# Five weight buffers, a later half of the first weights, and two pairs of heads in rounded parts

## The chip, the cores and the metric

The kernel runs on one core of a Trainium2 chip. The metric is the time of one launch in microseconds (us) as the device measures it; several runs are taken and their median is given. A profiled execution is a run of its own, and its time and its span (from the first to the last instruction) stand beside the median.

## The reference

Causal attention with a decay, for 4 batches, 8 heads, 576 rows and a head size of 64, and behind it two dense layers over all 2304 tokens (model width 512, hidden width 2048):

```python
scores = scale * np.matmul(q, k.transpose(0, 1, 3, 2))
cum = np.cumsum(np.log(np.clip(f, 0.0001, 1.0)), axis=-1)
decay = cum[:, :, :, None] - cum[:, :, None, :]
scores = np.where(causal, -1000000000.0, scores + decay)
attn = softmax(scores)
x = np.matmul(attn, v)            # then (tokens, 512)
x = np.maximum(x @ w_in, 0.0) ** 2 @ w_out
x = elu(x @ w_in2) @ w_out2
```

All of it is in float32.

## The kernel before, in words

**Two ways to multiply.** TensorE multiplies float32 as it is ("plain"), or two rounded parts of each operand: a high part in the rounded type F32R and the rest. With parts, a product is two or three matmuls over the parts. Making the parts costs copies and subtractions on the other engines.

**Attention.** The rows of a batch are cut at row 256. Kind "A" of a pair of heads is rows 0 to 255, kind "4" the last 64 rows of both heads together, and kind "B" rows 256 to 511 (with the last 64 rows joined in at the product with v). `todo` (lines 632 to 639) is the list of these items. For batch 0 (`SPLIT`) all eight A items come first, then for each of the four pairs the items 4, B, B; for the other batches each pair is A, A, 4, B, B. For an item `soft` makes the scores on TensorE, the row minimum of the negated scores on VectorE (line 315) and the exponential on ScalarE (line 318); one item later `outs` transposes (line 379) and multiplies with v (lines 383 and 386). The decay comes in as up to four more rows of q and k, taken from the tile `ca` for the first 256 rows and from `aug`, a table in DRAM, for the others (`aug_rows`, line 259).

**Batch 0 is plain** (`PLAIN`, lines 44 and 225). `fetch_plain` (line 232) brings the operands straight to where TensorE reads them: for A one `rawA` tile per pair (lines 237 to 242, three buffers of tag `raw`, so the fourth pair waits for the first), with two small transfers of decay rows from `ca` (line 240); for B a `rawB` and a `rawC` tile. `load_head` (line 266) has nothing to do for batch 0. For other batches `fetch_head` brings `raw` (800 KB, line 230), and `load_head` makes the parts `qk1` and `qk2` and `vv`: copies on ScalarE, VectorE and GpSimd, subtractions on GpSimd (`ENG`, line 46).

**The first dense layer** is done in two halves of the hidden width. During attention, `unit(u)` (line 572) computes the first half for 256 tokens; unit 0 can start when the A items of batch 0 are stored, and `moe_step` lets out one piece at a time by a credit per item (`PACE`, `COST`). Its weights, 8 slices of `w_in` and then 8 of `w_out`, are loaded by `load_w` (line 128): a transfer of 512 KB into one of two buffers `raws_w` (line 135), an Abs on ScalarE (line 141), four steps on VectorE that round a 64-bit number to float32 (lines 142 to 145; the tile is `wt`), then the high part on ScalarE (line 146) and the low part on GpSimd (line 147, `WL`). `W_AT` (line 36) says how many of these 16 weights are let out at each item.

**The order.** The kernel is written as a loop over the items (line 688). At item i it fetches for items up to i + 4 (`FETCH`), loads up to i + 2 (`AHEAD`), then weights, then scores, then the product with v of the item before, with pieces of the dense layer between. A planner orders the instructions of each engine by this order and by its own estimate of when operands are there, so an instruction whose operands are ready can be placed ahead of an earlier one that waits; a buffer is given out when its last reader is done. All transfers go out from SyncE's queue (SP), in one order. From the end of attention (`at.close()`, line 732) the rest of the first layer and the second layer follow.

Of the kernel before, what the change touches and what calls it, by code (L numbers as in the profile page):

```python
# [10 lines left out]
F32 = mybir.dt.float32  # L11
F32R = mybir.dt.float32r
I32 = mybir.dt.int32
# [3 lines left out]
B, H, S, D = 4, 8, 576, 64  # L17
# [7 lines left out]
RAW = QW + S  # L25
ALL = RAW + 5 * D
# [6 lines left out]
W_MAX = float(np.uint32(0x47EFFE00).view(np.float32))  # L33
PACE = (1.4, 0.9, 1.85, 1.75)
COST = {'A': 0.7, '4': 1.1, 'B': 1.7}
W_AT = (1, 1, 1, 1, 1, 1, 1, 1, 2, 2, 2, 2)
W_FIRST = 0
AHEAD = 2
FETCH = 4
LAG = 1  # L40
# [1 line left out]
SPLIT = (0,)  # L42

PLAIN = (0,)
CP = {'pA': 'a', 'pB': 'av', 'xA': 'a', 'xB': 'a'}
ENG = {'qk': 'aaa', 'ql': 'ppp', 'kh': 'pvv', 'kl': 'ppp', 'vh': 'ppp', 'vl': 'ppp', 'xl': 'pv'}
NORM = 'ap'
# [4 lines left out]
DEPTH1 = 2  # L52
ORD2 = (3, 0, 1, 2, 4)
AUG0 = 2
AUG_AT = 3
DELAY = 0
MEM = "gpsimd"
# [7 lines left out]
def f32(ap):  # L65
    return ap.bitcast(F32)
# [10 lines left out]
def attention_then_moe_kernel(ctx, tc, first, firstv, plain, qkv, aug0, f, w1, w2, out):  # L77
    nc = tc.nc
# [46 lines left out]
    def less(dst, x, hi):  # L125
        nc.gpsimd.tensor_tensor(out=dst, in0=x, in1=f32(hi), op=ALU.subtract)  # L126

    def load_w(src, m, fc, wp, i, late):
        if i == 0:
            wslot[m, fc] = wp.tile([128, 2, 1024], F32R, tag=f"w{fc}", name=f"w{m}_{fc}")  # L130
        w = wslot[m, fc]
        if late:
            raw = xb.tile([128, 512, 2], I32, tag="wraw", name="wraw")
        else:
            raw = raws_w[:, n_raw[0] % 2]
            n_raw[0] += 1
        nc.sync.dma_start(out=raw, in_=src[fc, i].bitcast(I32).rearrange("p (n t) -> p n t", t=2))
        lo, hi = raw[:, :, 0], raw[:, :, 1]
        t = xa.tile([128, 512], I32, tag="o", name="wt")
        wh, wl = (w[:, r, i * 512:(i + 1) * 512] for r in range(2))  # L140
        nc.scalar.activation(out=f32(t), in_=f32(hi), func=AF.Abs)  # L141
        nc.vector.tensor_scalar(f32(t), f32(t), W_MIN, W_MAX, op0=ALU.max, op1=ALU.min)  # L142
        nc.vector.tensor_scalar(t, t, 3, 0x3FFFFFFF, op0=ALU.logical_shift_left, op1=ALU.bitwise_and)
        nc.vector.scalar_tensor_tensor(t, hi, -0x40000000, t, op0=ALU.bitwise_and, op1=ALU.bitwise_or)
        nc.vector.scalar_tensor_tensor(t, lo, 29, t, op0=ALU.logical_shift_right, op1=ALU.bitwise_or)  # L145
        nc.scalar.activation(out=wh, in_=f32(t), func=AF.Copy)
        minus(WL[late][i], wl, f32(t), wh)

# [30 lines left out]
    nc.sync.dma_start(out=fr, in_=f)  # L179
    x0 = xa.tile([128, 2 * NC, CH], F32R, tag="xu", name="x0")  # L180
    raws_w = xa.tile([128, 2, 512, 2], I32, tag="xu", name="raws_w")
    qk2s = [a1.tile([128, RAW], F32R, name=f"qk2_{i}") for i in range(BUFS["qs"])]
    mz = a1.tile([128, 512], F32, name="mz")
    m4 = a1.tile([128, 288], F32, name="m4")
    ptA = [[a1.tile([128, 512], F32R, name=f"ptA{s}{t}") for t in range(2)] for s in range(2)]
# [29 lines left out]
    for k in range(2):  # L215
        mask(m4[64 * k:64 * k + 64, 224:288], [[-1, 64]])

    n_load = [0]

    raws = {}  # L220

    pairs = {}

    def fetch_head(b, h, part):
        if b in PLAIN:
            fetch_plain(b, h, part)
            return
        raw = ab.tile([128, ALL], F32, tag="raw", name="raw", bufs=BUFS["raw"])
        raws[b, h, part] = raw
        nc.sync.dma_start(out=raw, in_=qkv[b, h])  # L230

    def fetch_plain(b, h, part):
        g = b * H + h
        k = h % 2
        if part == "A":
            if k == 0:
                t = ab.tile([128, ALL], F32, tag="raw", name="rawA", bufs=BUFS["raw"])
                nc.sync.dma_start(out=t[0:64, 0:1024], in_=first[h // 2])
                for i in range(2):
                    nc.sync.dma_start(out=t[64:68, 512 * i:512 * i + 512], in_=f32(ca[g + i:g + i + 1]))  # L240
                nc.sync.dma_start(out=t[:, 1024:1280], in_=firstv[h // 2])
                pairs[b, h // 2] = t
            t = pairs[b, h // 2]
            raws[b, h, part] = Plain(t, 512 * k - Q0, 512 * k + 256, t[:, 1024 + 128 * k:1152 + 128 * k].rearrange("p (j d) -> p j d", d=D))
            return
        if k == 0:
            t = ab.tile([128, ALL], F32, tag="raw", name="rawB", bufs=BUFS["raw"])
        else:
            t = hd.tile([128, RAW], F32, tag="qk1", name="rawC", bufs=BUFS["qs"])
        nc.sync.dma_start(out=t[0:64, 0:RAW], in_=plain[h])  # L250
        nc.sync.dma_start(out=t[64:68, 0:RAW], in_=aug[g])
        if k == 0:
            v = t[:, RAW:ALL]
        else:
            v = hd.tile([128, 5 * D], F32, tag="vv", name="vp", bufs=BUFS["vv"])
        nc.sync.dma_start(out=v, in_=qkv[b, h, :, RAW:ALL])
        raws[b, h, part] = Plain(t, 0, QW, v.rearrange("p (j d) -> p j d", d=D))

    def aug_rows():
        cp, cn = (ab.tile([32, 2, S - 256], F32R, tag="eb", name=t, bufs=BUFS["eb"]) for t in ("cp", "cn"))  # L260
        split_c(cp, cn, slice(256, S))
        for rows, c0, src in ((slice(0, 2), Q0, ca[:, 0:2, 0:256]), (slice(2, 4), QW, ca[:, 2:4, 256:512]),
                              (slice(0, 2), 0, cp[:, :, 0:256]), (slice(0, 2), Q4, cp[:, :, 256:]), (slice(2, 4), QW + 256, cn)):
            nc.sync.dma_start(out=aug[:, rows, c0:c0 + src.shape[2]], in_=f32(src))

    def load_head(b, h, part):
        q0, q1, k1, js = {"F": (0, QW, S, 5), "A": (Q0, QW, 256, 2), "B": (0, Q0, S, 5)}[part]
        w = "ABF".index(part)
        raw = raws.pop((b, h, part))
        if b in PLAIN:  # L270
            return raw
        v0 = QW + 256 if part == "A" else RAW
        vr = raw[:, v0:v0 + js * D].rearrange("p (j d) -> p j d", d=D)
        qk1 = hd.tile([128, RAW], F32R, tag="qk1", name="qk1", bufs=BUFS["qs"])
        qk2 = qk2s[n_load[0] % len(qk2s)]
        n_load[0] += 1
        kc = slice(QW, QW + k1)
        qc = slice(q0, q1)
        g = b * H + h
        if part == "A":  # L280
            ac = slice(Q0, QW + 256)
            copy(ENG["qk"][w], qk1[:, ac], raw[:, ac])
        else:
            ac = slice(0, RAW)
            if part == "F":
                copy(ENG["qk"][w], qk1, raw[:, ac])
            else:
                copy(ENG["qk"][w], qk1[:, qc], raw[:, qc])
                copy(ENG["qk"][w], qk1[:, kc], raw[:, kc])
        if part == "A":  # L290
            nc.sync.dma_start(out=f32(qk2[64:68, ac]), in_=f32(ca[g:g + 1]))
        else:
            nc.sync.dma_start(out=f32(qk2[64:68, ac]), in_=aug[g, :, ac])
        minus(ENG["ql"][w], qk2[0:64, qc], raw[0:64, qc], qk1[0:64, qc])
        if ENG["kh"][w] == "d":
            nc.sync.dma_start(out=f32(qk2[0:64, kc]), in_=f32(qk1[0:64, kc]))
        else:
            copy(ENG["kh"][w], qk2[0:64, kc], f32(qk1[0:64, kc]))
        minus(ENG["kl"][w], qk1[64:128, kc], raw[64:128, kc], qk1[64:128, kc])
        vv = hd.tile([128, 5, 2 * D], F32R, tag="vv", name="vv", bufs=BUFS["vv"])  # L300
        copy(ENG["vh"][w], vv[:, 0:js, 0:D], vr)
        minus(ENG["vl"][w], vv[:, 0:js, D:2 * D], vr, vv[:, 0:js, 0:D])
        return qk1, qk2, vv
# [306 lines left out]
    def drain(gen):  # L610
        for _ in gen:
            pass
# [46 lines left out]
    wl = weights(1, w1, wa, range(8), False, True)  # L659

    wait = [0]

    def moe_step():
        for u in range(NU):
            if units[u] is None:
                continue
            if not started[u] and not ready(u):
                return False
            if not started[u] and u:
                if wait[0] < DELAY:  # L670
                    wait[0] += 1
                    return False
            started[u] = True
            wait[0] = 0
            if HOLD is not None and len(trail) > HOLD:
                with tc.issue_after(trail[-1 - HOLD].ins):
                    left = next(units[u], "end") != "end"
            else:
                left = next(units[u], "end") != "end"
            if left:  # L680
                return True
            units[u] = None
        return False

    credit = 0.0
    for _ in range(W_FIRST):
        next(wl)
    for i in range(len(todo) + LAG):
        if i == AUG0:
            nc.sync.dma_start(out=aug, in_=aug0)  # L690
        if i == AUG_AT:
            aug_rows()
        while fetches and fetches[0][0] <= i + FETCH:
            fetch_head(*fetches.pop(0)[1:])
        while loads and loads[0][0] <= i + AHEAD:
            load(*loads.pop(0)[1:])
        if i < len(todo):
# [217 lines left out]
```

## Time and profile before

| what | value |
|---|---|
| median of 3 runs (lowest to highest) | 1060.36 us (1059.25 to 1060.42) |
| profiled execution: its time, its span | 1061.57 us, 1059.8 us |
| mean granted TensorE clock | 0.998 |
| busy in the span: TensorE, its weight loads | 1027.7 us (97%), 873.6 us (82%) |
| busy in the span: VectorE, ScalarE, GpSimd | 621.3, 491.8, 228.2 us |
| moved by DMA | 115.48 MB, 109 GB/s over the span |

The profiled execution lies 1.2 us above the median of the runs. PE is TensorE's matmuls, PEld its weight loads, DVE VectorE, ACT ScalarE, POOL GpSimd, SP SyncE; SPq is an issue on SyncE's queue. A plain float32 matmul stands as two records in the trace. The end of a matmul is modelled, so in a run of matmuls the distance from one group's start to the next group's start tells more than the duration of one.

### The profile page before, as it was taken

Reading aid. Unit: us, or ns where it says so; the run is one execution under the profiler, and the core shown is the slowest. Engines: PE = TensorE matmul, PEld = TensorE weight load, DVE = VectorE, ACT = ScalarE, POOL = GpSimd, SP = SyncE. Lnnn points to the kernel's source line nnn. Section 1 sums busy time; section 2 is a strip of 40 time slices with the busy share of each in tenths; the row PEclk is TensorE's granted clock in tenths of the full one; section 3 lists DMA queues with packets and bytes.
Section 4 is the critical chain, followed back from the end, with each engine's and each line's share of the span. In section 5 each row is a group of like instructions: output and inputs, shape, how many; then the busy total and the mean of one; then the engine's idle time right before and its main releaser. Section 6 shows DMA issues by size and latency. Waiting matters only on the chain.

```text
span 1059.8 us, 15463 instructions
## 1 busy us (share of the span) xinstructions
PE 1027.7 (97%) x5696; PEld 873.6 (82%) x5696; DVE 621.3 (59%) x1363; ACT 491.8 (46%) x1055; POOL 228.2 (22%) x261
## 2 busy tenths in 40 slices
PE   4799999999999999999999999999999999999998
PEld 2567788899999998889988888888888888888897
DVE  5785468766776537868884278943433433343353
ACT  3675687887787634435453154521222222222232
POOL 4456477685777210000000000000000000000000
PEclk9999999999999999999999999999999999999999
DMA  8663534444441164454757236302100300200010
GB/s 225 179 192 110 192 108 148 157 142 160 142 142 49 43 197 135 139 162 148 232 183 229 80 119 239 119 1 78 42 1 1 119 1 1 70 11 1 0 41 20
DMA packets 60060, 115.48 MB, mean 109 GB/s; under 512 B 7296, under 2 KB 34688, under 8 KB 59968
## 3 DMA queue, kind: packets, MB, share of 16 engines
q1 hardware_dynamic: 59984, 114.49, 33.8%
q8 instruction: 45, 0.74, 0.3%
q14 instruction: 31, 0.25, 0.1%
HBM read 87.37 MB, written 27.69 MB: 109 GB/s over the span
## 4 chain that ended last, share of the span: by engine, by line
PE 89%; DMA 3%; ACT 3%; DVE 2%; issue 1%; SPq 1%; POOL 1%; ACTq 0%; POOLq 0%
PE O L159 32%; PE pH L159 32%; PE o L159 6%; PE ph L159 6%; PE pt L379 4%; PE pv L386 3%; DMA raws_w<-in_w_dram 3%; PE s L311 2%; PE s L312 2%; PE pv L383 2%; PE s L307 1%; ACT eb L318 1%; PE pr L379 1%; ACT qk L117 1%; DVE wt L145 1%
## 5 line engine op out<-in xcount | busy, mean ns | idle before, releaser
L159 PE MATMUL pH<-xu,w 128*128 128x512 f32 (+1 forms) x1632 | 354.0, 367 | 0.0
L159 PEld LDWEIGHTS pH<-xu,w 128*128 128x128 f32 x1632 | 283.0, 188 | 55.3
L159 PE MATMUL O<-w,gh 128*128 128x512 f32 x576 | 179.0, 394 | 0.0
L557 ACT ACTIVATE g<-g 128x512 f32<-128x512 f32 (+1 forms) x80 | 47.0, 589 | 196.8 <-DVE g L556 196.6
L159 PEld LDWEIGHTS O<-w,gh 128*128 128x128 f32 x576 | 107.2, 188 | 24.7
L159 PE MATMUL O<-gh,w 128*128 128x512 f32 (+1 forms) x448 | 122.0, 362 | 0.0
L113 DVE TENSOR_TENSOR gl<-g,gh 128x512 fp32r<-128x512 f32 (+1 forms) x136 | 85.2, 627 | 54.1 <-ACT gh L559 44.4
L159 PE MATMUL O<-w,gl 128*128 128x512 f32 x288 | 111.3, 392 | 0.0
L556 DVE TENSOR_SCALAR g<-pH 128x512 f32<-128x512 f32 (+1 forms) x80 | 51.0, 637 | 101.7 <-PE pH L159 101.5
L159 PEld LDWEIGHTS O<-gh,w 128*128 128x128 f32 x448 | 79.8, 189 | 14.2
L126 POOL TENSOR_TENSOR qk<-raw,qk 64x704 fp32r<-64x704 f32 (+1 forms) x48 | 78.6, 1637 | 20.1 <-ACT qk L117 14.9
L159 PE MATMUL O<-gl,w 128*128 128x512 f32 (+1 forms) x224 | 79.4, 363 | 0.0
L558 DVE SCALAR_TENSOR_TENSOR g<-g,pH 128x512 f32<-128x512 f32 (+1 forms) x80 | 50.7, 634 | 45.7 <-ACT g L557 45.4
L159 PE MATMUL o<-gh,w 128*128 128x256 f32 x384 | 75.0, 290 | 0.0
L559 ACT ACTIVATE gh<-g 128x512 fp32r<-128x512 f32 (+1 forms) x80 | 47.0, 589 | 56.0 <-DVE g L558 56.0
L159 PE MATMUL ph<-xu,w 128*128 128x256 f32 x480 | 68.5, 291 | 1.8 <-DMA xu<-x 1.5
L141 ACT ACTIVATE wt<-wraw 128x512 f32<-128x512 f32 x48 | 32.1, 670 | 76.8 <-DMA wraw<-in_w_dram 67.6
L159 PEld LDWEIGHTS O<-w,gl 128*128 128x128 f32 x288 | 54.1, 188 | 12.4
L159 PEld LDWEIGHTS ph<-xu,w 128*128 128x128 f32 x480 | 61.9, 194 | 2.7 <-DMA xu<-x 2.0
L159 PEld LDWEIGHTS o<-gh,w 128*128 128x128 f32 x384 | 60.1, 191 | 0.5 <-ACT e L318 0.2
L548 ACT ACTIVATE gh<-g 128x512 fp32r<-128x512 f32 (+1 forms) x80 | 46.6, 584 | 26.9 <-DVE g L547 23.6
L142 DVE TENSOR_SCALAR wt<-wt 128x512 f32<-128x512 f32 x64 | 28.2, 441 | 50.1 <-ACT wt L141 49.8
(132 smaller groups left out, 1696.0 us busy)
## 6 DMA issues: line engine op xcount, KB each, us to landing
wraw<-in_w_dram SPq DMA_DIRECT2D x48, 512.0 KB
raw<-in_qkv_dram SPq DMA_DIRECT2D x24, 800.0 KB
xu<-x SPq DMA_DIRECT2D x20, 512.0 KB
raws_w<-in_w_dram SPq DMA_DIRECT2D x16, 512.0 KB
x<-xs SPq DMA_DIRECT2D x16, 320.0 KB
xu<-x SPq DMA_DIRECT2D x20, 256.0 KB
x<-yh SPq DMA_DIRECT2D x16, 256.0 KB
x<-yl SPq DMA_DIRECT2D x16, 256.0 KB
```

The source lines that it names most:

```text
L113: nc.vector.tensor_tensor(dst, x, f32(hi), op=ALU.subtract)
L126: nc.gpsimd.tensor_tensor(out=dst, in0=x, in1=f32(hi), op=ALU.subtract)
L141: nc.scalar.activation(out=f32(t), in_=f32(hi), func=AF.Abs)
L142: nc.vector.tensor_scalar(f32(t), f32(t), W_MIN, W_MAX, op0=ALU.max, op1=ALU.min)
L159: nc.tensor.matmul(out=dst, lhsT=l, rhs=r, start=first and i == 0, stop=last and i == n - 1, skip_group_check=skip)
L379: seen[0] = nc.tensor.transpose(dst, src, ident[:, c0:c0 + 128])
L386: seen[0] = nc.tensor.matmul(out=dst, lhsT=hh[2][:, J, :], rhs=hl[i], start=first and i == 0, stop=last and i == 1)
L548: nc.scalar.activation(out=gh[:, 0:n], in_=g[:, 0:n], func=AF.Copy)
L556: nc.vector.tensor_scalar(g[:, 0:n], h[:, 0:n], 0.0, None, op0=ALU.min)
L557: nc.scalar.activation(out=g[:, 0:n], in_=g[:, 0:n], func=AF.Exp)
L558: nc.vector.scalar_tensor_tensor(g[:, 0:n], g[:, 0:n], -1.0, h[:, 0:n], op0=ALU.add, op1=ALU.max)
L559: nc.scalar.activation(out=gh[:, 0:n], in_=g[:, 0:n], func=AF.Copy)
```

## The change

- The 16 first weights get five buffers instead of two: the two of `raws_w` and three that share the tag `qk2` with the heads' second tile. Five transfers are started at item 0 (`stage`), and each weight starts the transfer of the fifth after it once VectorE has read it.
- `W_AT` lets out four weights, not eight, in the A items, none in items 4 to 7, and two at each of items 8 to 13. Whatever is left is let out ahead of step 9 of the units.
- B of pairs 2 and 3 of batch 0 (heads 4 to 7) goes by rounded parts, as in the other batches; pairs 0 and 1 stay plain (`PLAIN_B`).
- The fourth `rawA` comes into a buffer of tag `qk1` instead of one of the three of tag `raw`.
- The decay rows of `rawA` go out from ScalarE's queue instead of SyncE's.
- `aug` is filled in two portions: batch 0 at items 2 and 3, the other batches at item 8.

```diff
-W_AT = (1, 1, 1, 1, 1, 1, 1, 1, 2, 2, 2, 2)
-W_FIRST = 0
+W_AT = (1, 1, 1, 1, 0, 0, 0, 0, 2, 2, 2, 2, 2, 2)
+PLAIN_B = 2
+AUG1 = 8
...
+    staged = []
+    to_stage = [(fc, i) for i in range(2) for fc in range(8)]
+
+    def stage():
+        if not to_stage:
+            return
+        fc, i = to_stage.pop(0)
+        n = n_raw[0] % 5
+        n_raw[0] += 1
+        raw = raws_w[:, n] if n < 2 else a1.tile([128, 512, 2], I32, tag="qk2", name="wraw1", bufs=3)
+        nc.sync.dma_start(out=raw, in_=w1[fc, i].bitcast(I32).rearrange("p (n t) -> p n t", t=2))
+        staged.append(raw)
...
-            raw = raws_w[:, n_raw[0] % 2]
-            n_raw[0] += 1
-        nc.sync.dma_start(out=raw, in_=src[fc, i].bitcast(I32).rearrange("p (n t) -> p n t", t=2))
+            raw = staged.pop(0)
...
+        if not late:
+            stage()
         nc.scalar.activation(out=wh, in_=f32(t), func=AF.Copy)
...
-        if b in PLAIN:
+        if b in PLAIN and (part == "A" or h // 2 < PLAIN_B):
...
-                t = ab.tile([128, ALL], F32, tag="raw", name="rawA", bufs=BUFS["raw"])
+                if h // 2 < BUFS["raw"]:
+                    t = ab.tile([128, ALL], F32, tag="raw", name="rawA", bufs=BUFS["raw"])
+                else:
+                    t = hd.tile([128, RAW], F32, tag="qk1", name="rawA", bufs=BUFS["qs"])
...
-                    nc.sync.dma_start(out=t[64:68, 512 * i:512 * i + 512], in_=f32(ca[g + i:g + i + 1]))
+                    nc.scalar.dma_start(out=t[64:68, 512 * i:512 * i + 512], in_=f32(ca[g + i:g + i + 1]))
...
-        qk2 = qk2s[n_load[0] % len(qk2s)]
-        n_load[0] += 1
+        qk2 = a1.tile([128, RAW], F32R, tag="qk2", name="qk2", bufs=3)
...
+            n_step[0] += 1
+            if n_step[0] == 9:
+                drain(wl)
...
-            nc.sync.dma_start(out=aug, in_=aug0)
+            nc.sync.dma_start(out=aug[0:H], in_=aug0[0:H])
+        if i == AUG1:
+            nc.sync.dma_start(out=aug[H:], in_=aug0[H:])
...
+        if i == 0:
+            for _ in range(5):
+                stage()
```

## Rows read from the trace of the kernel before

**Rows 1.** Busy time by stretch: PE, PEld, DVE, ACT, POOL, clock, DMA share, GB/s.

```profile
0.00:13.70 13.70, 0.04 (x1) 0.07 (x1) 6.28 (x14) 4.78 (x6) 5.90 (x23) 1.00 0.73 220
13.70:47.10 33.40, 25.68 (x87) 17.25 (x87) 23.24 (x60) 18.81 (x54) 14.48 (x15) 1.00 0.73 191
47.10:89.10 42.00, 40.61 (x210) 26.64 (x209) 38.52 (x87) 29.42 (x69) 22.83 (x21) 1.00 0.60 173
89.10:133.00 43.90, 43.51 (x265) 31.92 (x265) 17.35 (x59) 25.16 (x59) 24.40 (x26) 1.00 0.50 163
133.00:180.00 47.00, 43.80 (x325) 41.53 (x325) 36.38 (x112) 39.20 (x101) 38.92 (x43) 0.96 0.37 120
180.00:1059.80 879.80, 874.05 (x4815) 756.20 (x4813) 499.50 (x1036) 374.47 (x767) 121.73 (x134) 1.00 0.30 98
```

**Rows 2.** The chain that ended last, in order of time: start, us, what.

```profile
17.47 6.08 DMA raws_w<-in_w_dram
23.63 5.72 DMA raws_w<-in_w_dram
```

**Rows 3.** The timeline, first 50 us: start, us, engine, line, operation, idle before.

```profile
4.73 0.91 SPq L137 DMA_DIRECT2D raws_w<-in_w_dram  x2
...
7.47 4.41 SPq L240 DMA_DIRECT2D rawA<-ca  x6
...
13.66 3.75 PE L307 MATMUL s<-rawA 68*128 68x256 f32 x8 [13.66 <-DMA rawA<-ca]
...
31.88 2.08 PE L307 MATMUL s<-rawA 68*128 68x256 f32 x4
...
40.30 1.13 PE L307 MATMUL s<-rawA 68*128 68x256 f32 x4
...
47.09 0.75 PE L307 MATMUL s<-rawB 68*128 68x288 f32 x2
```

**Rows 4.** Busy time of the tile wt's instructions by stretch: DVE, ACT, POOL.

```profile
0.00:47.10 47.10, 19.99 (x30) 9.74 (x15) 9.52 (x7) 1.00 0.73 199
47.10:92.00 44.90, 28.21 (x35) 10.77 (x17) 12.81 (x9) 1.00 0.59 170
```

**Rows 5.** The chain in order of time, 105 to 156 us: net TensorE durations.

```profile
105.05 1.46 PE s L307 x6
...
118.61 1.50 PE s L307 x4
...
123.83 1.22 PE pv L383 x4
...
126.68 0.14 PE s L311
...
127.77 0.58 PE pv L383 x4
...
129.38 0.24 PE s L311
...
154.01 0.88 PE pv L386 x6
...
155.21 0.38 PE pv L386 x4
```

**Rows 6.** GpSimd's groups by shape, 89.1 to 160 us: busy, mean ns, idle before.

```profile
L126 POOL TENSOR_TENSOR qk<-raw,qk 64x704 fp32r<-64x704 f32 x7 | 12.8, 1823 | 3.7 <-ACT qk L117 3.7
L126 POOL TENSOR_TENSOR qk<-raw,qk 64x576 fp32r<-64x576 f32 x7 | 10.1, 1438 | 0.5
...
L126 POOL TENSOR_TENSOR vv<-raw,vv 128x320 fp32r<-128x320 f32 x5 | 4.6, 917 | 0.2
L119 POOL TENSOR_SCALAR vv<-raw 128x320 fp32r<-128x320 f32 x6 | 3.0, 494 | 12.4 <-PE pv L383 5.5 <-DMA raw<-in_qkv_dram 5.0 <-PE pv L386 1.8
```

**Rows 7.** VectorE's groups by shape, 0 to 160 us: the rounded parts.

```profile
L121 DVE CAST qk<-qk 64x576 fp32r<-64x576 f32 x7 | 5.4, 778 | 6.1 <-ACT qk L117 6.1
...
L376 DVE TENSOR_TENSOR p<-pt,p 128x320 fp32r<-128x320 f32 x6 | 2.9, 480 | 0.0
```

**Rows 8.** The timeline of PE, 76 to 78 us.

```profile
76.78 0.65 PE L307 MATMUL s<-rawB 68*128 68x288 f32 x2
```

More of the change, by code (lines that the diff above doesn't have):

```diff
@@ L134, in load_w @@
         else:
-            raw = raws_w[:, n_raw[0] % 2]
-            n_raw[0] += 1
-        nc.sync.dma_start(out=raw, in_=src[fc, i].bitcast(I32).rearrange("p (n t) -> p n t", t=2))
+            raw = staged.pop(0)
+        if late:
+            nc.sync.dma_start(out=raw, in_=src[fc, i].bitcast(I32).rearrange("p (n t) -> p n t", t=2))
         lo, hi = raw[:, :, 0], raw[:, :, 1]
@@ L181, in attention_then_moe_kernel @@
     raws_w = xa.tile([128, 2, 512, 2], I32, tag="xu", name="raws_w")
-    qk2s = [a1.tile([128, RAW], F32R, name=f"qk2_{i}") for i in range(BUFS["qs"])]
     mz = a1.tile([128, 512], F32, name="mz")
@@ L216, in attention_then_moe_kernel @@
         mask(m4[64 * k:64 * k + 64, 224:288], [[-1, 64]])
-    n_load = [0]
     raws = {}
@@ L257, in fetch_plain, with aug_split, aug_rows @@
         raws[b, h, part] = Plain(t, 0, QW, v.rearrange("p (j d) -> p j d", d=D))
-    def aug_rows():
+    def aug_split():
         cp, cn = (ab.tile([32, 2, S - 256], F32R, tag="eb", name=t, bufs=BUFS["eb"]) for t in ("cp", "cn"))
         split_c(cp, cn, slice(256, S))
+        return cp, cn
+    def aug_rows(g, cp, cn):
         for rows, c0, src in ((slice(0, 2), Q0, ca[:, 0:2, 0:256]), (slice(2, 4), QW, ca[:, 2:4, 256:512]),
                               (slice(0, 2), 0, cp[:, :, 0:256]), (slice(0, 2), Q4, cp[:, :, 256:]), (slice(2, 4), QW + 256, cn)):
-            nc.sync.dma_start(out=aug[:, rows, c0:c0 + src.shape[2]], in_=f32(src))
+            nc.sync.dma_start(out=aug[g, rows, c0:c0 + src.shape[2]], in_=f32(src[g]))
     def load_head(b, h, part):
@@ L269, in load_head @@
         raw = raws.pop((b, h, part))
-        if b in PLAIN:
+        if isinstance(raw, Plain):
             return raw
@@ L661, in attention_then_moe_kernel @@
     wait = [0]
+    n_step = [0]
     def moe_step():
@@ L685, in attention_then_moe_kernel @@
     credit = 0.0
-    for _ in range(W_FIRST):
-        next(wl)
     for i in range(len(todo) + LAG):
         if i == AUG0:
-            nc.sync.dma_start(out=aug, in_=aug0)
+            nc.sync.dma_start(out=aug[0:H], in_=aug0[0:H])
+        if i == AUG1:
+            nc.sync.dma_start(out=aug[H:], in_=aug0[H:])
         if i == AUG_AT:
-            aug_rows()
+            cpn = aug_split()
+            aug_rows(slice(0, H), *cpn)
+        if i == AUG1:
+            aug_rows(slice(H, B * H), *cpn)
         while fetches and fetches[0][0] <= i + FETCH:
             fetch_head(*fetches.pop(0)[1:])
+        if i == 0:
+            for _ in range(5):
+                stage()
         while loads and loads[0][0] <= i + AHEAD:
```

## The prediction

> **What bounds the kernel now.** I read the busy time by stretch first [rows 1]. From 180 us on PE is busy for 874.05 of 879.8 us, and the change edits nothing there. So what is won before 180 us should reach the end one to one, and the search is for time that PE loses ahead of it. There are four stretches to read. Up to 13.7 us PE does nothing. From 13.7 to 47.1 (the A items) it is busy for 25.68 of 33.4 us, and part of that is at the lower of its two clock levels: the column says 1.00, but the same group of four score records took 2.08 us at 31.88 and 1.13 us at 40.30 [rows 3]. From 47.1 to 89.1 (pairs 0 and 1 of the B items, and weights) VectorE is busy for 38.52 of 42 us: it sets the pace. From 89.1 to 133 (pairs 2 and 3) PE is busy for 43.51 of 43.9 us with VectorE at 17.35: PE sets the pace.
>
> The chain then shows why the A items are slow: it stands on the weights' transfers at 17.47 and 23.63 us, 6.08 + 5.72 = 11.8 us [rows 2]. Two buffers mean that a transfer starts only when the weight two before it has been read, and ScalarE and VectorE, which run in order, wait for it with attention queued behind.
>
> **The change part by part.**
>
> *The first scores.* The six issues of decay rows from `ca` begin at 7.47 us, 4.41 / 6 = 0.74 us each, and the first score waits for them until 13.66 [rows 3], behind two weights (4.73 us) and the filling of `aug` on the same queue. They move to ScalarE, which is busy for 4.78 of the first 13.7 us [rows 1], so the eight issues (eight times 0.74 = 5.9 us, six of them early) cost nothing there. If only the issue counted, the pair's two rows are out by 7.47 + 1.48 = 8.95: gain 4.7 us. If they had to wait until all that SP issued before is in, that is three pairs of `rawA` (3 x 0.39 MB) and now five weights (5 x 0.52 MB), 3.8 MB at the 220 GB/s of this stretch [rows 1], 17.3 us behind a start at about 1.2: 18.5 us, a loss of 4.8. I take 11.2, **-2.5 us**, about midway from the issue to the old value, because the small rows leave a queue in which most of that data stands ahead of them.
>
> By the Trainium skill (DMA: Bandwidth & Descriptors, Issuing engines are not separate DMA queues) transfers issued by several engines share the same DMA engines, and a second issuing engine saves only the sequencer's time to issue. The same page (Queues, rings and completion order) says that an engine takes turns between the queues it has work for. No row here shows two queues. By the first rule alone the backlog stays and the sum would lose up to 7.3 us; it stands among the rivals.
>
> *The A items.* Weights of the first 47.1 us cost VectorE 19.99 us for 30 instructions, four to a weight, and 28.21 for 35 later; over all 48.2 / 16 = 3.0 us a weight, and ScalarE 20.5 / 16 = 1.3 us [rows 4]. Four fewer weights take 12 us from VectorE's 23.24 and 5.2 from ScalarE's 18.81 in this stretch [rows 1]. The 11.8 us of transfers [rows 2] go from the chain, since five are started ahead. What is late next is PE itself at its lower level: 2.08 against 1.13 us for a group [rows 3] means about 1 us a group, and I give back 4.4 us for the groups that still run so and for the longer way from score to product. **-7.4 us**: the stretch becomes 26. Bounds: 0 (the items are held by something else), and -13 (20 us, near what is left of PE's 25.68 if most of it runs at the higher level). The fourth `rawA` no longer waits for the first; the waits it could cause lie in the same stretch and are not counted again.
>
> *Weights among pairs 0 and 1.* The four weights come here: 12 us more on the engine that sets the pace. But the planner places what is ready, and with five transfers ahead weights can be taken into VectorE's gaps in the A items, which are then 26 - 11.2 = 14.8 us wide: room for all four. Bounds 0 and +12; I take half, **+6 us**.
>
> *Pairs 2 and 3 in rounded parts.* On PE, per head [rows 5]: plain scores of 512 and 384 columns 1.50 us; rounded two products of 0.24 and, by columns, two of 0.18: 0.84. Plain products with v three of 1.22 / 2 = 0.61 and 0.58: 2.41; rounded 0.88 + 0.38 = 1.26. Per pair, the last rows: plain four of 1.46 / 3 = 0.49, 1.95; rounded eight of 0.14, 1.12. So a pair saves 2 x (0.66 + 1.15) + 0.83 = 4.45 us, and both 8.9, all in the stretch where PE sets the pace. What it adds: GpSimd per head two subtractions (448 columns, by columns 1.82 x 448 / 704 = 1.16; 576 columns 1.44), 0.92 and 0.49 for v: 4.0, in all 16 us [rows 6]. VectorE per head one copy of 0.78 and five operations of about 0.48 more, less two copies it no longer makes, about 2.2, in all 9 us [rows 7], against 26 us idle in that stretch. Transfers: 0.8 MB a head instead of 0.5, 1.2 MB more, against 163 GB/s where the first stretch bore 220. GpSimd is the tight one: 24.4 + 16 = 40.4 us of work in a stretch that would be 35 long [rows 1]. About half can go ahead of 89 us, where GpSimd is busy for 22.83 of 42. Its highest share so far is 38.92 of 47, 83%, in the next stretch, which loses 3.2 us of PE. I give back 3: **-5.9 us**, bounds -8.9 and 0.
>
> *The rest.* The two portions of `aug` move the same bytes in five more issues on SP, which has them at an item where PE is not waiting for SP; nothing, and with the cover gone a few issues of half a microsecond.
>
> Sum: -2.5 - 7.4 + 6 - 5.9 = **-9.8 us** on the profiled execution's 1061.57, so 1051.8; the median of the runs lies 1.2 lower: **1050.6 us**.
>
> **The rivals.**
> 1. *More of it.* All four weights go into the gaps (0 instead of +6) and GpSimd holds nothing up (-8.9 instead of -5.9): 1050.6 - 9 = 1041.6. For it speaks that five transfers are there early; against it GpSimd's share.
> 2. *GpSimd takes PE's place.* 16 us of new work fall in stretches where it is already at 24.4 and 38.92 [rows 1]; pairs 2 and 3 then gain nothing: 1050.6 + 5.9 = 1056.5.
> 3. *The decay rows wait for the backlog* in front of the first score, +4.8 instead of -2.5: 1050.6 + 7.3 = 1057.9. This is what the first rule of the Trainium skill cited above (DMA: Bandwidth & Descriptors) would make of it.
> 4. *Slower: the rounded heads wait for weight buffers.* The second tile of heads 4 to 7 comes from the three buffers that weights 12 to 14 hold, and those are freed by VectorE only at the end of the weights. If none of the four weights finds a gap, that end is 89.1 - 9.9 + 12 = 91.2, then about 5 us of copies and subtractions: the first rounded score at 96, where pair 2 began at 76.78 [rows 8]. From there to 133 it took 56.2 us before, now 47.3; less some 5.6 us of the dense unit's work that PE can do meanwhile, 137.7 against 133: +4.7, so 1065. It decides when the first rounded score is later than about 91. For it: the buffers are shared as written. Against it: the loads are placed ahead of their items, and the first of these buffers is freed some weights before the last.
> 5. *The change does not do what it says*, because the planner puts the weights where it likes: then the A items keep eight weights and only prefetching is left; this lies between the forecast and 1056 and has its chance in the forecast's.
>
> **How the numbers follow.** The forecast (1044 to 1056) has 0.57, rival 1 0.15, rival 2 0.08, rival 3 0.07, rival 4 0.13. About 0.2%, 2.1 us, is what a measurement can tell here. Faster by more: the forecast, rivals 1 and 2 and a small part of 3, 0.81; within it: the rest of 3, 0.06; slower 0.13. The range, 1038 to 1061, takes in the bounds of single terms and leaves out rival 4 and the case in which all terms come out best. The forecast's own is 1044 to 1056.
>
> **What would show it.** The first score near 11 us; no wait on weights' transfers in the chain between 17 and 30 us; the first B score near 37; VectorE nearly full up to about 85 us; per pair 4.45 us less on PE for pairs 2 and 3; the same work from 180 us on, only earlier. It is wrong if the first B score is still later than 44, if GpSimd is above nine tenths while PE idles, or if PE's first rounded score comes after 91.

## The result and the profile after

The changed kernel takes **1066.51 us** (median of 20 runs, 1061.47 to 1071.38) against 1061.3 for the kernel before in as many runs on the same chips: ratio **1.0052 [1.004, 1.0064]**, so slower, where 1050.6 was forecast. Its profiled execution took 1062.75 us (span 1061.0), near the lowest of its runs, so its trace explains a time some 4 us under the median.

The busy time by stretch, changed kernel (columns as in [rows 1]):

```profile
0.00:13.70 13.70, 0.93 (x2) 0.84 (x3) 4.65 (x10) 3.45 (x4) 5.89 (x23) 1.00 0.85 266
13.70:47.10 33.40, 28.29 (x105) 18.19 (x103) 27.97 (x79) 24.48 (x66) 15.30 (x16) 0.95 0.84 237
47.10:89.10 42.00, 36.97 (x212) 26.92 (x213) 40.42 (x63) 27.13 (x64) 31.57 (x32) 0.96 0.44 151
89.10:133.00 43.90, 36.66 (x244) 31.86 (x243) 32.02 (x85) 32.63 (x77) 31.70 (x33) 0.96 0.49 164
133.00:180.00 47.00, 44.04 (x322) 42.26 (x321) 33.41 (x108) 36.60 (x96) 35.40 (x39) 0.93 0.37 121
```

The page's busy line, changed kernel:

```profile
PE 1021.1 (96%) x5696; PEld 876.6 (83%) x5696; DVE 639.0 (60%) x1379; ACT 499.2 (47%) x1071; POOL 243.9 (23%) x277
```

PE does 6.6 us less than before (1021.1 against 1027.7) and idles 7.8 us more (39.9 us of its span against 32.1). From 47.1 to 133 us it is busy for 73.6 of 85.9 us, where it was 84.1 [rows 1]. VectorE works 40.42 of 42 us and, new, still 32.02 of the next 43.9, though in the first of these stretches it completes 63 instructions where 87 stood before.

PE's timeline, changed kernel:

```profile
12.77 5.46 PE L326 MATMUL s<-rawA 68*128 68x256 f32 x12 [12.77 <-DMA rawA<-ca]
...
24.20 1.13 PE L326 MATMUL s<-rawA 68*128 68x256 f32 x4
...
35.93 0.75 PE L326 MATMUL s<-rawB 68*128 68x288 f32 x2 [0.70 <-DMA aug<-cn]
...
94.39 0.50 PE L330 MATMUL s<-qk 128*128 128x512 f32 x1 [2.88 <-DVE nm L334]
```

In this run the head of the kernel went as forecast: the first B score is at 35.93 us, 11.2 us earlier than in [rows 3]. All of that is lost again before the first rounded score of 512 columns at 94.39. Its plain form stood 16.6 us earlier in the kernel before (PE's timeline there):

```profile
77.75 1.02 PE L307 MATMUL s<-rawB 68*128 68x512 f32 x2
```

The chain of waits in that stretch, changed kernel:

```profile
73.72 2.75 DVE wt L159
...
79.66 4.48 DVE wt L157
...
87.89 5.73 DVE qk L123
```

It runs through single instructions of VectorE. The last one is a copy of 64x576 that took 0.78 us on average before [rows 7]. What GpSimd does meanwhile (its timeline, changed kernel):

```profile
87.87 1.15 POOL L128 TENSOR_TENSOR qk<-raw,qk 64x448 fp32r<-64x448 f32 x1 [2.09 <-DVE wt L160]
88.98 1.27 POOL L128 TENSOR_TENSOR w<-wt,w 128x512 fp32r<-128x512 f32 x1
90.21 1.29 POOL L128 TENSOR_TENSOR gl<-g,gh 128x512 fp32r<-128x512 f32 x1
91.46 0.85 POOL L128 TENSOR_TENSOR vv<-raw,vv 128x320 fp32r<-128x320 f32 x1
92.27 1.03 POOL L566 TENSOR_TENSOR g<-g 128x512 f32<-128x512 f32 x1
```

Five instructions stand without a gap from 87.87 to 93.30, at about their usual durations; VectorE's copy starts with the first and ends 0.3 us after the last. GpSimd's work for heads 4 to 7 is part of this run, and so is the weights' own subtraction (`w<-wt,w`).

A second wait stands beside this one, and it is the one of the prediction's rival 4. The second tile of a rounded head lies in a buffer that a weight (`wraw`) holds first. VectorE's copy into the tile starts each time within 0.1 us of the end of the weight step that reads such a buffer last (VectorE's timeline, changed kernel; the third copy is the one at 87.89):

```profile
67.96 1.67 DVE L160 SCALAR_TENSOR_TENSOR wt<-wraw,wt 128x512 int32<-128x512 int32 x1
69.67 1.01 DVE L123 CAST qk<-qk 64x576 fp32r<-64x576 f32 x1
...
77.12 0.80 DVE L160 SCALAR_TENSOR_TENSOR wt<-wraw,wt 128x512 int32<-128x512 int32 x1
77.95 1.00 DVE L123 CAST qk<-qk 64x576 fp32r<-64x576 f32 x1
...
87.11 0.68 DVE L160 SCALAR_TENSOR_TENSOR wt<-wraw,wt 128x512 int32<-128x512 int32 x1
```

So the first product of pair 2's first scores stands on PE at 64.05 us, and the second, which reads that tile, only at 80.00:

```profile
64.05 0.29 PE L330 MATMUL s<-qk 128*128 128x288 f32 x1
...
80.00 0.59 PE L331 MATMUL s<-qk 68*128 68x288 f32 x1
```

### The profile page after: what moved, and what is told of

The parts are those of the page before. It is cut to its first block, busy times and chain, and to the rows that moved or that the text cites. A ratio compares the mean times of both kernels' runs of the same rounds, so it can differ in the third digit from the quotient of the medians.

```text
span 1061.0 us, 15574 instructions
## 1 busy us (share of the span) xinstructions
PE 1021.1 (96%) x5696; PEld 876.6 (83%) x5696; DVE 639.0 (60%) x1379; ACT 499.2 (47%) x1071; POOL 243.9 (23%) x277
## 4 chain that ended last, share of the span: by engine, by line
PE 88%; DVE 6%; ACT 3%; DMA 1%; issue 1%; POOL 1%; DVEq 0%; ACTq 0%; POOLq 0%
PE O L176 32%; PE pH L176 32%; PE o L176 6%; PE ph L176 5%; PE pv L405 4%; PE pt L398 4%; PE s L330 2%; PE s L331 2%; DVE wt L157 1%; DVE wt L159 1%; PE s L326 1%; DVE qk L123 1%; ACT eb L337 1%; DVE wt L160 1%; ACT qk L119 1%
## 5 line engine op out<-in xcount | busy, mean ns | idle before, releaser
L128 POOL TENSOR_TENSOR qk<-raw,qk 64x576 fp32r<-64x576 f32 (+2 forms) x56 | 89.7, 1602 | 24.2 <-ACT qk L119 16.6
L156 ACT ACTIVATE wt<-wraw 128x512 f32<-128x512 f32 x57 | 38.1, 670 | 78.5 <-DMA wraw<-in_w_dram 69.1
L157 DVE TENSOR_SCALAR wt<-wt 128x512 f32<-128x512 f32 x64 | 35.1, 548 | 41.9 <-ACT wt L156 28.6
```

## The experiments

Medians; ratios, with their 95% intervals, are to the kernel before in the same batch. By these intervals a difference between two experiments is uncertain by some 2 to 3 us. "All plain" means that all four pairs of batch 0 are plain, as before.

### Which part of the change loses

**e1_all_plain**: the change without the rounded pairs.

```diff
-PLAIN_B = 2
+PLAIN_B = 4
```

> The changed kernel with all four pairs of batch 0 plain again (no rounded parts, buffers and weights as changed). Port theory (GpSimd's work for heads 4 to 7 blocks VectorE): VectorE's CAST and wt operations stay under 2 us each, the A items still end about 11 us earlier than in the kernel before, PE has 8.9 us more to do; the time comes out at 1050 to 1058, faster than both. Weight theory (four more weights after the A items are the loss): VectorE still sets the pace up to 90 us and the time stays at 1062 or more.

Measured: 1054.61 us, 0.9957 [0.9935, 0.9979]. By these ten runs the rest of the change gains 6.7 us and rounding costs 12. But six of them lie at 1053.9 to 1054.8 and four at 1059.1 to 1062.7, and more runs (e7 below) make it 3.4 and 8.6.

**e2_rounded_only**: the kernel before, with `PLAIN_B = 2` alone.

> The kernel before with pairs 2 and 3 of batch 0 in rounded parts and nothing else; heads 4 to 7 have second tiles of their own, the weights two buffers. Port theory: GpSimd's work still meets the weights on VectorE, operations of 2 us and more on VectorE, 1060 to 1067. Buffer theory (heads 4 to 7 wait for weight buffers): no such wait here, first rounded score before 85 us, 1052 to 1056.

Measured: 1059.36, 0.9982 [0.9968, 0.9996]. Rounding gains 2 us of the 5.9 forecast here. This kernel has neither the earlier head nor the shared buffers, so the loss hangs on one of them or on both.

**e4_two_buffers**: the changed kernel with the two old weight buffers alone.

```diff
-        n = n_raw[0] % 5
+        n = n_raw[0] % 2
...
-        raw = raws_w[:, n] if n < 2 else a1.tile([128, 512, 2], I32, tag="qk2", name="wraw1", bufs=3)
+        raw = raws_w[:, n]
...
-            for _ in range(5):
+            for _ in range(2):
```

> The changed kernel with only the two old weight buffers, so heads 4 to 7 share nothing with weights. Buffer theory: first rounded score before 88 us, 1054 to 1061. Port theory: the long VectorE operations stay and the time stays at 1062 to 1070; the A items lose part of their gain.

Measured: 1065.68, 1.0039 [1.0021, 1.0057]. The wait for weight buffers goes: pair 2's first two products stand at 65.39 and 65.85 us and its score of 512 columns at 74.58, 20 us earlier than in the changed kernel. The time stays. But the edit also gives up part of the head (the first B score is at 41.57, not 35.93), so it does not show that the shared buffers (rival 4 of the prediction) cost nothing; they are not the whole cause.

**e6_weights_early** and **e7_plain_weights_early**: the old `W_AT`, in the changed kernel and in e1.

```diff
-W_AT = (1, 1, 1, 1, 0, 0, 0, 0, 2, 2, 2, 2, 2, 2)
+W_AT = (1, 1, 1, 1, 1, 1, 1, 1, 2, 2, 2, 2)
```

> The changed kernel with the weights let out as before (eight in the A items, eight in items 8 to 11). Collision theory (GpSimd's work for heads 4 to 7 meets weights on VectorE because the weights come later): fewer weights left when heads 4 to 7 are loaded, 1056 to 1062, faster than the changed kernel by 4 or more. If rounding itself is the loss, 1064 to 1068 as the changed kernel.

> E1 (all plain) with the weights let out as before: what is left of the change is the five buffers, the fourth buffer and the decay rows on ScalarE's queue. If the later weights were what won E1's 6.7 us, this is at 1060; if the buffers won it, it stays at 1053 to 1056.

Measured: 1065.15, 1.0048 [1.0024, 1.0072], and 1059.04, 0.9978 [0.9954, 1.0002], with its lowest runs at 1053.9 as in e1. The list has next to no effect: by 47.1 us VectorE has done 33 weight instructions in the changed kernel and 33 in e6, against 30 before [rows 4], and in e1 and e7 VectorE's instructions have the same order up to 120 us. The planner places a weight when it is there. So e1, e7 and e11 (below) are one kernel in effect. Their 21 runs go from 1053.9 to 1065.93 with a median of **1057.95**; this is what "the plain kernel" means from here on.

**e13_ca_sync**: e1 with the decay rows on SyncE's queue again.

```diff
-                    nc.scalar.dma_start(out=t[64:68, 512 * i:512 * i + 512], in_=f32(ca[g + i:g + i + 1]))
+                    nc.sync.dma_start(out=t[64:68, 512 * i:512 * i + 512], in_=f32(ca[g + i:g + i + 1]))
```

> All four pairs plain (e1_all_plain), with the small decay rows of the first 256 rows issued by SyncE again, not by ScalarE. If moving them is what brought the first score forward (12.8 us against 13.7), it goes back to 13.7 or later, and the time rises by about 1 us, to 1055.6; if ScalarE's 7 us of issuing delayed its first weight steps by more than SyncE gained, it becomes faster by about 2 us; nothing moves if the pairs' own 260 KB set the first score.

Measured: 1058.71 (1055.5 to 1069.55), 1.0 [0.9969, 1.003]. The first score moves from 12.8 to 14.05 us, 1.3 us later; the runs spread too far to say whether the whole does.

### That it is GpSimd's new work

**e3_parts_off_gpsimd**: the changed kernel with the parts of heads 4 to 7 made by VectorE and ScalarE.

```diff
-ENG = {'qk': 'aaa', 'ql': 'ppp', 'kh': 'pvv', 'kl': 'ppp', 'vh': 'ppp', 'vl': 'ppp', 'xl': 'pv'}
+ENG = {'qk': 'aaa', 'ql': 'pvp', 'kh': 'pav', 'kl': 'pvp', 'vh': 'pap', 'vl': 'pvp', 'xl': 'pv'}
```

> The changed kernel with the parts of heads 4 to 7 made by VectorE (three subtractions) and ScalarE (two copies) instead of GpSimd and VectorE. Port theory: no VectorE operation over 2 us, the weights end before 90 us, 1052 to 1060. Buffer theory: the first rounded score stays near 94 us and the time within 1062 to 1068.

Measured: 1057.52, 0.9969 [0.9952, 0.9987]: 9 us back, though VectorE has more to do. Its instructions for `wt` take 43.2 us, against 53.7 in the changed kernel.

**e9_keys_on_scalar**: only the copy that waited 5.73 us goes to ScalarE (`'kh': 'pav'`).

> The changed kernel with one copy per head (64x576, the keys' high part, the CAST that took up to 5.73 us on VectorE) moved from VectorE to ScalarE; GpSimd's work is untouched. Port theory: the four blocked copies go (6 us of waiting on VectorE), 1058 to 1063. If GpSimd's own slowness for the heads is the loss, no gain: 1065 to 1068.

Measured: 1063.08, 1.0007 [0.9981, 1.0033]: some 3 us. `wt` now takes 55.2 us: the wait is now in the weights' steps.

**e5_idle_gpsimd_work**: e1, and GpSimd makes heads 4 to 7's parts though nobody reads them.

```diff
+            if part == "B" and h >= 4:
+                d = a1.tile([128, RAW], F32R, tag="qk2", name="qk2", bufs=3)
+                less(d[0:64, 0:Q0], raw.t[0:64, 0:Q0], raw.t[0:64, 0:Q0])
+                less(d[0:64, QW:RAW], raw.t[0:64, QW:RAW], raw.t[0:64, QW:RAW])
+                less(d[0:64, QW:RAW], raw.t[0:64, QW:RAW], raw.t[0:64, QW:RAW])
+                vr = raw.v
+                dv = d[:, 0:5 * D].rearrange("p (j d) -> p j d", d=D)
+                copy("p", dv, vr)
+                less(dv, vr, vr)
```

> E1 (all plain) with GpSimd's work for heads 4 to 7 added and read by nobody: per head a subtraction of 64x448, two of 64x576, a copy and a subtraction of 128x320, into a buffer of the shared tag. GpSimd was idle for 18 of the 42 us there. Port theory: VectorE's two-number steps of the weights stretch to 2 us and more, and the time rises by 4 us or more over E1 (1059 and up). If GpSimd's work only matters by the heads that wait for it, nobody waits here and the time stays within 1.5 us of E1.

Measured: 1063.95, 1.0026 [1.001, 1.0042]: 9.3 us over e1's ten runs and **6.0 over the plain kernel**, from GpSimd's work alone, though nobody waits for it.

**e10_fills**: as e5, but after one copy GpSimd only fills, and reads nothing.

```diff
+                copy("p", dv, raw.v)
+                for _ in range(4):
+                    nc.gpsimd.memset(f32(d[:, 0:1120]), 0.0)
```

> The five reading operations of GpSimd of e5_idle_gpsimd_work are replaced by one copy and four fills of 1120 columns, about 5 us per head as there, in the same tiles and at the same place of GpSimd's queue: fills only write SBUF. If a fixed order (GpSimd's queue, the three buffers of tag qk2) costs the time, it stays at e5's 1064. If GpSimd's reads lock VectorE's two-input steps alone, lines 159 and 160 of the weights (in this kernel 165 and 166) fall back to the durations of e1_all_plain and the tensor_scalar steps stay long: some 1058. If every access of GpSimd counts, VectorE's steps stay as long as in e5 (wt 54 us in all, against 46) and it stays near 1064. Back at 1054.6 with wt at 46 us would say that the fills disturb nobody, and that neither queue nor buffers cost anything.

Measured: 1062.1, 1.0011 [0.9998, 1.0024]: 4.2 over the plain kernel. GpSimd is busy for 244.8 us in all, as in e5, so the two differ in what GpSimd does and not in how long.

### By which way: a lock, or the queue

Two ways were left. (a) GpSimd's accesses to SBUF hold up VectorE's instructions. (b) The weights' subtraction stands behind the new work in GpSimd's queue, so that the tile `wt` comes free late. The same edit takes (b) away in seven kernels; the subtraction goes to VectorE:

```diff
-WL = ('pp', 'vv')
+WL = ('vv', 'vv')
```

**e12_plain_lows_vector**: e1 with that edit.

> All four pairs plain (e1_all_plain), and the low part of the early weights' rows (the subtraction, 16 of 128x512) on VectorE in place of GpSimd. If GpSimd's use of SBUF is what stretches VectorE's weight steps, they fall below e1's means (1152, 762, 607 and 842 ns), which pays for most of the 16 subtractions of about 0.7 us that VectorE gets: 1054 to 1058. If VectorE's own work bounds the stretch up to 89 us, the 11 us come on top and half of them show: about 1060.

Measured: **1049.49 (1047.57 to 1053.77), 0.99 [0.9878, 0.9922]**, the quickest so far, 8.5 us under the plain kernel (5.1 under e1's ten runs), and it beats both kernels.

**e14_rounded_lows_vector**: the changed kernel with that edit.

> The changed kernel (1066.5) with the weights' low parts subtracted on VectorE, not GpSimd; the rounded heads' work stays on GpSimd. The same edit won 5 us with all pairs plain (1054.6 to 1049.5). (a) VectorE's steps are stretched by GpSimd's accesses: the loss of the rounded pairs stays, some 1061. (b) the weights waited in GpSimd's queue: that loss goes as well, 1050 to 1054. Something between, 1057 to 1058, would say that both count about alike.

Measured: 1057.21, 0.997 [0.9958, 0.9983]: 9.3 us better than the changed kernel. The edit wins 8.5 with plain pairs too (5.1 by e1's ten runs), so a share of the queue in rounding's own loss does not stand clear of the noise here. 7.7 above e12 are left, and those are not the weights' place in the queue.

**e15_idle_work_lows_vector** and **e17_fills_lows_vector**: e5 and e10 with that edit.

> All pairs plain, low parts of the weights on VectorE (e12_plain_lows_vector, 1049.5), and GpSimd does heads 4 to 7's work with nobody reading it, as in e5_idle_gpsimd_work. (a) the reads and writes of GpSimd stretch VectorE: +9 us as there, near 1058, with single weight steps of VectorE up to 3 us. (b) it was the queue: within 2 us of 1049.5.

> The same with fills in place of the reading operations (e10_fills), low parts of the weights on VectorE. (a) half of e15's loss, by VectorE's steps in e10_fills: near 1054. (b) within 2 us of 1049.5. If it costs the same 7 us as in e10_fills, neither reads nor the weights' place in the queue are the cause, and the buffers of tag qk2 that the idle work shares with the staged weights are the next suspect.

Measured: e15 1055.69, 0.9958 [0.9939, 0.9977], **6.2 above e12**; e17 **1048.07** (1047.08 to 1048.37), 0.9882 [0.9858, 0.9905], **nothing above e12**. The edit wins 14.0 us beside fills (e10 to e17), 8.3 beside reads (e5 to e15). So what the fills cost in e10 went with the weights' place in the queue, and what reads still cost in e15 does not. GpSimd is busy about as long in both (226.7 and 224.6 us), and both put their work into the buffers that they share with the weights, so neither its time nor the buffers make the difference: the reads do. Busy time of the tile `wt`'s instructions, 0 to 130 us (columns: stretch, DVE, ACT, POOL where it has any, clock, DMA share, GB/s), in e1:

```profile
0.00:130.00 130.00, 46.05 (x64) 20.23 (x32) 20.87 (x16) 1.00 0.62 183
```

in e5:

```profile
0.00:130.00 130.00, 54.73 (x64) 20.52 (x32) 21.59 (x16) 0.95 0.61 179
```

in e12 (VectorE has 16 instructions more):

```profile
0.00:130.00 130.00, 48.48 (x80) 20.60 (x32) 1.00 0.67 193
```

in e15:

```profile
0.00:130.00 130.00, 57.30 (x80) 20.76 (x32) 0.99 0.62 183
```

and in e17:

```profile
0.00:130.00 130.00, 50.26 (x80) 20.73 (x32) 1.00 0.64 194
```

Reads lengthen the same 64 or 80 instructions by 8.7 and 8.8 us (e5 over e1, e15 over e12), fills by 1.8 (e17 over e12; in e10, with the subtraction on GpSimd, it is 50.07 us, 4.0 over e1). Single instructions show the lock. The timeline of VectorE and GpSimd in e15:

```profile
84.84 1.57 POOL L128 TENSOR_TENSOR qk<-rawC 64x576 fp32r<-64x576 f32 x1
...
85.33 3.52 DVE L160 SCALAR_TENSOR_TENSOR wt<-raws_w,wt 128x512 int32<-128x512 int32 x1
...
86.37 1.03 POOL L575 TENSOR_TENSOR g<-g 128x512 f32<-128x512 f32 x1
87.37 2.48 POOL L128 TENSOR_TENSOR qk<-rawC 64x448 fp32r<-64x448 f32 x2
```

and in e17:

```profile
70.37 1.49 POOL L572 TENSOR_TENSOR g<-g 128x512 f32<-128x512 f32 x1
...
70.88 2.23 DVE L157 TENSOR_SCALAR wt<-wt 128x512 f32<-128x512 f32 x1
...
71.80 1.03 POOL L296 MEMSET qk<- 128x1120 f32 x1
...
78.97 3.25 POOL L296 MEMSET qk<- 128x1120 f32 x3
...
79.34 0.69 DVE L159 SCALAR_TENSOR_TENSOR wt<-raws_w,wt 128x512 int32<-128x512 int32 x1
79.95 0.68 DVE L115 TENSOR_TENSOR w<-wt,w 128x512 fp32r<-128x512 f32 x1
80.55 0.68 DVE L160 SCALAR_TENSOR_TENSOR wt<-raws_w,wt 128x512 int32<-128x512 int32 x1
```

Three steps with two inputs in SBUF run through three fills at their plain 0.68 us (79.34 to 81.23), where the same kind took 3.52 us beside four instructions that read. A step with one input (line 157, plain 0.42 us) waits for a read and for the fill behind it, until 73.11. The Trainium skill (SBUF — State Buffer, Who interferes with whom) states this: two SBUF inputs on VectorE meet GpSimd's reads, not its bare writes, and a copy, cast or tensor_scalar in a two-port mode meets both. The traces agree.

**e16_parts_and_lows_off**: e3 with that edit, so GpSimd has neither.

> The changed kernel with heads 4 to 7's parts on VectorE and ScalarE (e3_parts_off_gpsimd, 1057.5) and the weights' low parts on VectorE too. If GpSimd's part in the weights costs as much here as with plain pairs, 5 us come off: 1052.5, and rounding then costs 3 us against e12_plain_lows_vector. If VectorE, which has about 10 us of parts and 11 us of subtractions more, now sets the pace up to 90 us, it stays at 1057 or gets worse. Under 1049 would say that rounding pays once GpSimd is out of the way.

Measured: 1054.0, 0.9933 [0.9914, 0.9952], 4.5 above e12. Rounding does not pay even with both of GpSimd's jobs taken away. Two stretches of the busy time suggest one reason (columns as in [rows 1]), first of e12:

```profile
47.10:89.10 42.00, 42.00 (x248) 30.56 (x246) 36.58 (x85) 30.69 (x66) 18.51 (x18) 1.00 0.57 155
89.10:133.00 43.90, 42.61 (x265) 32.66 (x265) 23.79 (x84) 28.78 (x73) 23.23 (x27) 1.00 0.52 170
```

then of e16:

```profile
47.10:89.10 42.00, 38.33 (x208) 28.55 (x208) 39.50 (x82) 32.63 (x71) 13.64 (x12) 0.84 0.51 164
89.10:133.00 43.90, 40.69 (x293) 36.77 (x293) 35.43 (x110) 38.99 (x96) 30.67 (x34) 1.00 0.50 168
```

The parts are made while weights are still rounded, on a VectorE at 39.5 of 42 us; PE is busy for 3.7 us less there, at a granted clock of 0.84, and for 1.9 less in the stretch that was to gain. The other reason that is left is the wait for weight buffers, which this kernel keeps: the copy into the first such tile starts at 70.46 us, when the weight step before it ends. No run tells the two apart.

**e19_pair3_lows_vector**: e12 with one pair rounded (`PLAIN_B = 3`).

> e12_plain_lows_vector (1049.5) with pair 3 alone in rounded parts. If the loss hangs on GpSimd's reads beside the weights, which end near 81 us there, pair 3's parts fall mostly behind them and the saving on TensorE (4.4 us by the prediction's own count for one pair) shows at least in part: 1046 to 1049. If any rounded pair costs its share, half of 7.7 us: 1053.

Measured: 1053.55, 0.9933 [0.9916, 0.9949]: +4.1, about half of two pairs' 7.7. Its parts were not made behind the weights either: GpSimd's subtractions for them begin at 65.39 us, and the weights end after 80.

**e18_before_lows_vector**: the kernel before with that edit.

> The kernel before (1061) with the weights' low parts on VectorE. With all pairs plain and the change's first part that edit won 5 us, and the first part itself 6.7. If the two are independent: 1056. If the weights' buffers bound the kernel before, so that a shorter chain behind them only waits for the next load: 1059 to 1061.

Measured: 1060.52, 0.9996 [0.9986, 1.0005]: nothing. With two buffers the chain behind a weight is not what it waits for; the edit gains only beside the rest of the change (e12).

**e11_plain_again**: e1 once more, for a profile.

> The kernel of e1_all_plain once more, for its profile alone: its times lay at 1054 or at 1059 to 1062. Theory: the quicker ones are those in which TensorE reaches its upper clock level early (scores of 68x288 near 0.5 us in place of 1.0 by 25 us, as in the changed kernel), the slower ones those like the profile taken, with the lower level until after 40 us. A profile near 1054 with the level rising only after 40 us makes it wrong; one near 1060 with an early rise too.

Measured: 1057.95, with PE at its lower level until after 44 us, as in e1's first profile (1060.69). That agrees with the second half of the expectation's theory. No trace shows a run near 1054, so whether TensorE's level rises early in those stays open.

## Why the prediction was wrong

**The step that failed: pairs 2 and 3 in rounded parts, -5.9 us; about +9 measured** (8.6, the plain kernel against the changed one; 12 by e1's ten runs). The saving on PE is there at least in part: PE's busy time fell by 6.6 us, and in e16 it is 3.8 us under e12's, at a granted clock down to 0.84; the 8.9 was not measured by itself. What failed was where the cost falls. The prediction set GpSimd's 16 us and VectorE's 9 us against the idle time of 89 to 133 us, and let half of GpSimd's work go ahead of 89 us at no price, since GpSimd was idle for 19 of 42 us there. But that stretch is the one in which VectorE sets the pace, and GpSimd's instructions are not beside VectorE's: they hold them up. The copy of keys and the steps of the weights wait for whole runs of GpSimd's instructions. GpSimd's work alone costs 6.0 us (e5 against the plain kernel), and 6.2 with the weights out of GpSimd's queue (e15 against e12). Even without GpSimd, 4.5 us are left (e16): the parts' own work on VectorE in the same stretch, or the wait for weight buffers; that was not tried apart. "PE sets the pace from 89 to 133" was read rightly and used wrongly: work for a stretch is done ahead of it.

**The first scores, -2.5 us: about -0.9.** They come at 12.77 us, against 13.66 [rows 3] and a forecast of 11.2. The rows go out from 7.45 us on, as they did on SyncE's queue (7.47 [rows 3]), so the weights ahead of them had not held back their issue; they land 5.2 us later. On SyncE's queue the first score is 1.3 us later (e13). Neither end was met, and rival 3 (18.5 us) falls. Nor do the issues cost nothing on ScalarE: six take 7.20 us there, 1.2 each against 0.74, and its first weight step starts at 14.70 us, where it stood at 11.31 before.

**The A items, -7.4 us: more than that in the profiled run, for half of the reason and with luck.** The first B score was to be near 37 and is at 35.93, and the waits on weights' transfers [rows 2] have left the chain. But not fewer weights did it: VectorE does 27.97 us of work in this stretch, not 11. Five buffers did, and PE's clock. From the first score to the first B score it takes 33.4 us before, with two buffers and PE at its lower level up to 38 us; 28.0 in e1, with five buffers and the lower level until after 44 us; 28.0 in e4, with two buffers and the upper level from 25 us on; and 23.2 in the changed kernel, with five buffers and the upper level from 24 us on (1.13 us for four records). The kernels differ in more than these two things, so the halves are rough. The clock's half does not come with the change in every run: the plain kernel has the same head and in its three traces the lower level.

**Weights among pairs 0 and 1, +6 us: nothing moved.** `W_AT` does not hold weights back (e6), so rival 5 was true here. The terms but the rounding summed to -3.9, and the plain kernel gives -3.4 (e1's ten runs alone -6.7). That this agrees is partly luck: the weights' +6 came out at nothing, while the first scores gained 0.9 and, in the plain kernel's traces, the A items 5.4.

**The rivals.** Rival 2 (GpSimd takes PE's place, 1056.5) named the engine but not what it does: it put GpSimd as late, pairs 2 and 3 gaining nothing, and had no way below nothing. The term's bound of 0 was the error; a gain of nothing was taken as the worst. Rival 4 named the right sign, and its wait is in the trace, but not as it was priced: with the wait gone, the time stays (e4), and GpSimd's work costs 6 us without it (e5). It also counted from a wrong row: [rows 8] is not where pair 2 began, which was 7.5 us earlier (PE's timeline, kernel before):

```profile
69.26 0.65 PE L307 MATMUL s<-rawB 68*128 68x288 f32 x2
```

Of the signs that were to make the prediction wrong, one came: from 70 to 80 us GpSimd is busy for 9.43 of 10 us and PE for 8.14. The other two did not: the first B score is early, and the first rounded scores, of 288 columns, stand on PE from 64.05 us on, though those of 512 columns begin at 94.39.

## What to carry to other kernels

Idle time of GpSimd is not free room while VectorE sets the pace: count part of what GpSimd reads from SBUF there as VectorE's own time. Here 21 us of it (GpSimd 226.7 us in e15, 205.6 in e12) lengthened VectorE's weight steps by 8.8 us. A subtraction that VectorE waits for can be better placed on VectorE, even when VectorE is the full engine: 16 of 0.68 us gained 5 to 8.5 us here, though nothing in the kernel before (e18). Before work is moved into the shadow of a stretch, look when its inputs are made, not when its output is used.

## What the runs showed of the hardware that was not expected

- The wait is not for one instruction. A copy of VectorE that takes 0.51 us elsewhere in the same trace (at 102.74 us) waited through five of GpSimd's in a row (5.73 us), while GpSimd kept its usual durations.
- The times of one kernel lie in groups, and when PE reaches its upper level may be what parts them; that is not shown. e13's profiled run took 1069.55 us, 14 more than its quickest, with PE at its lower level (1.17 us for two scores of 288 columns) until after 64 us; in e12, another kernel, the same scores took 0.65 us from 37 us on. The clock column says 1.00 in both stretches: here the durations tell the level, not the column. e13, then e12, PE's timeline:

```profile
64.38 1.17 PE L326 MATMUL s<-rawC 68*128 68x288 f32 x2
```

```profile
37.86 0.65 PE L326 MATMUL s<-rawC 68*128 68x288 f32 x2
```
- In the changed kernel PE's clock falls in the middle of the work, each time behind idle time. From 74 to 78 us PE is busy for 2.1 of 4 us, and from 78 to 82 the granted clock is 0.56 to 0.59. It is idle from 91.5 to 94.4 us, and from 96 to 98 the clock is 0.50. In the 10 us from 90 on it is busy for 7.12 us at 0.83, where e12 has 10.00 at 1.00. The wait and the clock are then both paid for.
